# Last expert's sum in two half-column banks, and the first sixteen output rows taken straight from partial sums

## The chip, the core and the metric

The kernel runs on one core of a Trainium2 chip. A core has five engines with queues of their own: TensorE (PE: matmuls, with weight loads shown as PEld), VectorE (DVE), ScalarE (ACT), GpSimd (POOL) and SyncE (SP, which here only issues transfers). Matmul results go to PSUM, which has eight banks; everything else lies in SBUF. Sixteen transfer (DMA) engines move data between HBM and SBUF. The metric is the device time of one launch in microseconds (us); lower is better.

## What is computed

Two layers follow each other. The first is a gated recurrence over time, separately for each batch b and channel; the second a "soft mixture of experts" over all tokens of all batches:

```
B, S, D = 4, 5056, 256;  E = 8 experts, 4 slots each (32 slots), F = 1024
f = lb + (1 - lb) * sigmoid(f_logit)
h[t] = f[t] * h[t-1] + (1 - f[t]) * x[t]           # y = all h, [B*S, D]
logits = y @ phi                                    # [N, 32]
d = softmax of logits over the tokens
slot_input = d.T @ y                                # [32, D]
for e in range(8):
    hid = relu(slot_input[e] @ w1[e])               # [4, F]
    slot_out[e] = hid @ w2[e]                       # [4, D]
c = softmax of logits over the 32 slots
out = c @ slot_out                                  # [N, D], N = 20224
```

The output can't begin before slot_out is complete, since every output row is a mix of all 32 slots, and slot_out needs the last expert's w2.

## The kernel before

Nearly all of the span is one long pass over the input: 4 batches in groups of 512 time steps are loaded, gated (ScalarE), transposed (TensorE), scanned (VectorE), transposed back, and turned into exponentials of the logits, which stay in SBUF as `etall`: 128 partitions, 32 slots for each of the 4 batches, by 5056 time steps. The order of instructions on every engine is that in which the program is written (a manual schedule); a tile framework adds the waits. Weights are loaded by GpSimd's queue behind the input (`load_w`, L135), converted to bf16 on the way. The last w2 comes in two pieces: 6 of its 8 row blocks, then 2 (L144).

The part that the change touches begins after the pass.

- **Experts.** The 4 slots of an expert are rows of a 32-column block, since slots of all experts lie side by side. Eight row blocks (`fc`) of w2 are contracted one after the other. Experts 0 to 3 (L692 to L697) use `hid`, 32 columns wide: `fc % 4` picks one of four 32-row groups of PSUM, so that four matmuls can stand side by side in TensorE's array; the result is four partial sums, one in each row group. They are copied to `so4` (L699), and a matmul with `rep2` (L711), a 128x128 matrix of 4x4 identity blocks, adds the four groups up and leaves the sum four times, once in each group, as the output needs it (one copy of the slots for each batch). Experts 4 to 7 (L703 to L708) use `wide`, in which the 32 columns already stand four times; their matmuls are 128 columns wide and add into the same bank. `row_sums` (L407) and the reciprocals (L702, L716, L717) make the scale 1 / sum(c) of every output row. `spin` and `long_spin` (L150, L155) are matmuls whose result nobody reads; they keep TensorE busy.
- **slot_out and slot_bd.** When the last expert is in, VectorE copies the sum to bf16 as `slot_out` (L720). GpSimd multiplies it by two columns of `parity` into `slot_bd` (L722): for two batches at a time, each batch's slots in a block of their own, so that one matmul makes a row of both batches.
- **First output.** `pieces` (L765) makes the first 16 rows of batch 0's first block with `slot_out` (a "row" is 128 tokens, one on each partition): five transfers of 2, 2, 2, 4 and 6 rows, each row evicted from PSUM and scaled, half of them by ScalarE, half by VectorE. Then `by_rows` (L780) makes the last block, 7 rows, of two batches at a time with `slot_bd`, as tile `oc`: two transfers. `rest`, `whole` and `couple` make the remainder. All output transfers are issued by SP, in this order.

PSUM tiles of the first rows come from two pools, `psu` (2 banks) and `pfirst` (6 banks), by turns (`first_op`, L756). `ob_first` lies in a pool `ofirst` that is opened before the experts.

Of the kernel before, what the change touches and what calls it, by code (L numbers as in the profile page):

```python
# [9 lines left out]
F32 = mybir.dt.float32  # L10
# [8 lines left out]
def kernel(  # L19
# [148 lines left out]
    with tc.tile_pool(name="sp2", bufs=3) as sp2, \  # L168
# [433 lines left out]
        hid, wide = (ld.tile([P, 2, R, D], F32, name=i, tag="x_t") for i in ("hid", "wide"))  # L602
        hid = hid.rearrange("p u r d -> p (u r d)").bitcast(BF16)[:, ds(0, FC * E // 2 * NS)]
        wide = wide.rearrange("p u r d -> p (u r d)").bitcast(BF16)[:, ds(0, FC * E // 2 * P)]
        nc.gpsimd.memset(hid, 0.0)
        nc.gpsimd.memset(wide, 0.0)
        hid = hid.rearrange("p (f e s) -> p f e s", f=FC, s=NS)
        wide = wide.rearrange("p (f w b s) -> p f w b s", f=FC, b=B, s=NS)
# [29 lines left out]
    ob_first = ob_first[:, ds(0, wide_r * D)].rearrange("p (r d) -> p r d", d=D)  # L638

    with tc.tile_pool(name="ew", bufs=1) as ew, \  # L640
         tc.tile_pool(name="pm", bufs=2, space=PSUM) as pm, \
         tc.tile_pool(name="pbig", bufs=1, space=PSUM) as pbig:
# [27 lines left out]
        for q in range(E // Q):  # L670
            ht_ps = psu.tile([P, FC, P], BF16, name="ht_ps", tag="up")
            hi_v = his[q].rearrange("p (c f) -> p f c", f=FC)
            for fc in range(FC):
                nc.tensor.transpose(ht_ps[:, fc], hi_v[:, fc], ident)
            if q == 0:
                src = ht_ps.rearrange("p f (j s) -> p f j s", s=NS)[:, :, :, ds(0, SPE)]
                src = bass.AP(tensor=src.tensor, offset=src.offset,
                              ap=[list(src.ap[0]), [P, FC], [NS + SPE, Q], [1, SPE]])
                dst = hid[:, :, :, ds(0, SPE)]
                dst = bass.AP(tensor=dst.tensor, offset=dst.offset,  # L680
                              ap=[list(dst.ap[0]), [Q * NS, FC], [NS + SPE, Q], [1, SPE]])
                nc.scalar.copy(dst, src)
                continue
            for j in range(Q):
                s0 = (Q + j) * SPE
                src = ht_ps[:, :, ds(j * NS + s0, SPE)]
                copy = nc.scalar.copy if j % 2 == 0 else nc.vector.tensor_copy
                copy(wide[:, :, j, :, ds(s0, SPE)],
                     src.unsqueeze(2).broadcast_to([P, FC, B, SPE]))
        so4_ps = pm.tile([P, D], F32, name="so4_ps", tag="pm")  # L690
        for e in range(Q):
            for fc in range(FC):  # L692
                nc.tensor.matmul(so4_ps[ds(fc % 4 * NS, NS), :], hid[:, fc, e],
                                 w2_sb[e][:, fc],
                                 start=(e == 0 and fc < 4),
                                 stop=(e == Q - 1 and fc >= FC - 4),
                                 skip_group_check=True)  # L697
        so4 = ew.tile([P, D], F32, name="so4")
        nc.vector.tensor_copy(so4, so4_ps)  # L699
        so_ps = pm.tile([P, D], F32, name="so_ps", tag="pm")  # L700
        row_sums(1, range(4, 16))
        nc.vector.reciprocal(rrow[:, :wide_r], rs_ps[:, :wide_r])  # L702
        for j in range(Q):  # L703
            if j == 2:
                long_spin(tail[:, 1], 3)
            for fc in range(FC):
                nc.tensor.matmul(so_ps, wide[:, fc, j].rearrange("p b s -> p (b s)"),
                                 w2_sb[Q + j][:, fc], start=j == 0 and fc == 0,  # L708
                                 stop=j == Q - 1 and fc == FC - 1, skip_group_check=True)
            if j == 0:  # L710
                nc.tensor.matmul(so_ps, rep2, so4, start=False, stop=False,  # L711
                                 skip_group_check=True)
                row_sums(2)
            if j == 1:
# [186 lines left out]
```

## Time and profile before

| what | value |
|---|---|
| time, median of 3 runs | 196.53 us (196.46 to 196.62) |
| time of the profiled execution | 196.46 us |
| its span, first to last instruction | 194.7 us |
| busy: PE, DVE, ACT, POOL | 148.0, 142.1, 138.4, 102.5 us |
| HBM read, written | 58.23 MB, 20.71 MB |
| output transfers issued: five pieces, first oc, second oc | 143.36, 143.81, 144.29, 144.78, 145.82; 148.05; 150.35 us |
| slot_out copy (L720), slot_bd products (L722) | 0.42 us; 0.93 and 0.91 us |

The page of a profile shows busy times, the span in 40 slices (each digit is a busy share in tenths; PEclk is the granted TensorE clock; DMA is the transfer engines' share), and the chain of work that ended last, followed back from the last instruction. An answer of the timeline has start, length, engine, line, operation, tiles, shapes and count of each group of instructions, and in brackets how long the engine sat idle before it and what released it. SPq and POOLq are the queues that issue transfers. A window's row has its bounds and length, the busy time of PE, PEld, DVE, ACT and POOL with the instructions that were under way, then the granted clock, the transfer share and GB/s. Busy time of an engine that nobody waits for costs nothing.

### The profile page before, as it was taken

To read this page: it belongs to the slowest core of one execution; us is meant where nothing else is said; L and a number is where in the kernel's file an instruction comes from. 1 tells how busy PE (TensorE), PEld (TensorE's weight loads), DVE (VectorE), ACT (ScalarE), POOL (GpSimd) and SP (SyncE) were. 2 spreads that over 40 slices of the span, in tenths; PEclk is the share of its full clock that TensorE was granted. 3 is DMA by queue.
4 is the path that set the end of the run, shared out by engine and by line. 5 is a ranking of instruction groups with operands and counts; after the bars stand their busy time and mean duration, and the time that the engine had idled before them with its cause. 6 is when DMAs were issued, how large, how long until landed. Compare 5 with 4: busy or idle time off the path is not lost.

```text
span 194.7 us, 3260 instructions
## 1 busy us (share of the span) xinstructions
PE 148.0 (76%) x1216; PEld 105.2 (54%) x1216; DVE 142.1 (73%) x176; ACT 138.4 (71%) x192; POOL 102.5 (53%) x77
## 2 busy tenths in 40 slices
PE   0685686997989979898898976999696999980000
PEld 0474555685767758666685765667461764420000
DVE  2666899899799999999999999443178767770000
ACT  3687889799789998899998697421068688992000
POOL 2586877874998688884979977580030000000000
PEclk9999999699999999999999999999996555555555
DMA  5999999999999999999999999999939999999995
GB/s 200 418 434 423 428 428 421 431 431 356 373 426 426 405 338 423 426 428 344 391 412 398 269 221 213 214 215 214 177 149 425 432 447 431 431 431 431 431 431 222
DMA packets 11953, 70.75 MB, mean 363 GB/s; under 512 B 1297, under 2 KB 1682, under 8 KB 7458
## 3 DMA queue, kind: packets, MB, share of 16 engines
q1 hardware_dynamic: 9456, 62.13, 76.4%
q0 software_dynamic: 2480, 8.42, 21.6%
q8 instruction: 9, 0.15, 0.3%
q14 instruction: 6, 0.05, 0.1%
q10 hardware_dynamic: 2, 0.00, 0.0%
HBM read 58.23 MB, written 20.71 MB: 406 GB/s over the span
## 4 chain that ended last, share of the span: by engine, by line
PE 31%; DVE 23%; DMA 19%; ACT 6%; POOL 6%; issue 4%; SPq 1%; POOLq 1%; ACTq 0%; DVEq 0%
DVE h L334 16%; DMA w_t<-in_moe_w_dram 10%; PE op L829 7%; DMA w_sb<-in_moe_w_dram 6%; PE op L740 5%; POOL u_t L247 5%; PE hp L347 4%; PE up L266 4%; PE sp L251 4%; DMA f_t<-in_f_logit_dram 4%; DVE ht L366 3%; ACT s_t L236 3%; DVE oc L730 2%; PE lg L380 2%; PE slot_ps L185 1%
## 5 line engine op out<-in xcount | busy, mean ns | idle before, releaser
L247 POOL TENSOR_TENSOR u_t<-s_t,x_t 128x1024 bf16<-128x1024 bf16 (+1 forms) x39 | 82.3, 2127 | 21.7 <-ACT s_t L236 14.8
L334 DVE TENSOR_TENSOR_SCAN h<-a,h,up 128x512 bf16<-128x512 f32 x64 | 78.1, 1266 | 5.5 <-PE up L266 2.8
L236 ACT ACTIVATE s_t<-f_t 128x2048 bf16<-128x2048 f32 (+2 forms) x23 | 38.2, 1669 | 5.9 <-DMA f_t<-in_f_logit_dram 5.7
L347 PE MATMUL hp<-ident_f,h 128*128 128x128 f32 (+1 forms) x160 | 29.1, 305 | 7.4 <-DVE ht L366 4.7
L347 PEld LDWEIGHTS hp<-ident_f,h 128*128 128x128 f32 (+1 forms) x160 | 23.1, 206 | 16.4 <-DVE ht L366 9.3
L299 ACT ACTIVATE a<-sp,lbs 128x1024 f32<-128x1024 bf16 x28 | 29.7, 1114 | 2.2 <-PE sp L251 2.2
L251 PE MATMUL sp<-ident_f,s_t 128*128 128x128 f32 x144 | 21.4, 292 | 7.1 <-ACT s_t L236 5.7
L266 PE MATMUL up<-ident_f,u_t 64*128 64x64 f32 x224 | 21.2, 233 | 4.2 <-POOL u_t L247 4.0
L251 PEld LDWEIGHTS sp<-ident_f,s_t 128*128 128x128 f32 x144 | 17.4, 150 | 8.8 <-ACT s_t L236 6.7
L266 PEld LDWEIGHTS up<-ident_f,u_t 64*128 64x128 f32 x224 | 16.7, 141 | 8.9 <-POOL u_t L247 5.0
L366 ACT COPY ht<-hp 128x512 f32<-128x512 f32 (+1 forms) x21 | 12.2, 582 | 4.8 <-PE hp L347 4.8
L306 ACT ACTIVATE a<-sp,lbs 128x512 f32<-128x512 bf16 (+2 forms) x16 | 13.2, 867 | 2.6 <-PE sp L251 2.4
L185 PE MATMUL slot_ps<-rep,ident_f 128*128 128x256 f32 x42 | 13.8, 419 | 0.0
L366 DVE COPY ht<-hp 128x512 f32<-128x512 f32 (+1 forms) x19 | 12.7, 668 | 0.8 <-PE hp L347 0.8
L829 PE MATMUL op<-slot_bd,etall 64*128 64x512 bf16 x32 | 13.1, 626 | 0.0
L840 ACT ACTIVATE oc<-op,rrow 128x256 f32<-128x256 f32 x32 | 12.2, 486 | 0.8 <-PE op L829 0.3
L740 PE MATMUL op<-slot_out,etall 32*128 32x256 bf16 x64 | 12.6, 374 | 0.1
L834 DVE TENSOR_TENSOR oc<-op,rrow 128x1024 f32<-128x1024 f32 x8 | 9.7, 1223 | 3.3 <-PE op L829 3.3
L740 PEld LDWEIGHTS <-etall 32*128 32x128 bf16 x64 | 9.0, 153 | 3.9 <-issue 1.7
L734 ACT ACTIVATE ob<-op,rrow 128x256 f32<-128x256 f32 x24 | 9.4, 474 | 2.1 <-PE op L740 1.7
L380 PE MATMUL lg<-h,phi 128*32 128x512 bf16 (+1 forms) x80 | 10.5, 405 | 0.2 <-ACT et L404 0.2
L334 DVE TENSOR_TENSOR_SCAN h<-a,up 128x512 bf16<-128x512 f32 x8 | 9.3, 1208 | 1.6 <-PE up L251 0.9
(110 smaller groups left out, 170.0 us busy)
## 6 DMA issues: line engine op xcount, KB each, us to landing
f_t<-in_f_logit_dram SPq DMA_DIRECT2D x14, 1024.0 KB, 12.4
x_t<-in_x_dram SPq DMA_DIRECT2D x14, 1024.0 KB, 11.4
w_sb<-in_moe_w_dram POOLq DMA_DIRECT2D x14, 512.0 KB, 10.9
out_dram<-ob SPq DMA_DIRECT2D x3, 2048.0 KB, 9.7
f_t<-in_f_logit_dram SPq DMA_DIRECT2D x8, 512.0 KB, 8.6
x_t<-in_x_dram SPq DMA_DIRECT2D x8, 512.0 KB, 7.7
out_dram<-oc SPq DMA_DIRECT2D x1, 4096.0 KB, 13.9
out_dram<-oc SPq DMA_DIRECT2D x2, 2048.0 KB, 15.3
```

What stands on the lines that cost most here:

```text
L185: nc.tensor.matmul(slot_bank[:, 1], ident_f, wide_rep, start=first, stop=False, skip_group_check=True)
L236: nc.scalar.activation(s_t, f_t, ACT.Sigmoid, scale=-1.0)
L247: nc.gpsimd.tensor_tensor(uts[n][:, :r], s_t[:, :r], x_t[:, :r], ALU.mult)
L251: nc.tensor.transpose(ps[:, :, r], t[:, r].bitcast(F32), ident_f)
L266: nc.tensor.transpose(v[:, :, r], t(r)[k].bitcast(F32), ident_f[k, k])
L299: nc.scalar.activation(a, sp[:, :, :, :, o], ACT.Identity, scale=nomlb[:, ds(o, 1)], bias=1.0)
L334: nc.vector.tensor_tensor_scan(h[:, :T, o], decays[n // 2, o][:, n % 2, :T], up[:, :T, o], hs[number(g - 1, b)][:, ds(used(g - 1) - 1, 1), ...
L347: nc.tensor.transpose(hp[:n_p, r], hw[:, :n_p, r], ident_f)
L366: copy(hts[g][:n_p, b].rearrange("p r d -> p (r d)").bitcast(F32), hps.pop(n)[:n_p].rearrange("p r c -> p (r c)"))
L380: nc.tensor.matmul(lg[ds(b * NS, NS), :], phi[:, o], hs[number(g, b)][:, :T, o], start=o == 0, stop=o == DC - 1, skip_group_check=True)
L740: nc.tensor.matmul(op[:, j], ew[:, :, r + j], slot_out[ds(b * NS, NS)], start=True, stop=True, skip_group_check=True)
L829: nc.tensor.matmul(op[:, i_r].rearrange("p u d -> p (u d)"), ew[:, :, r + i_r], slot_bd[ds(j * 2 * NS, 2 * NS)].rearrange("s u d -> s (u d)"),
```

## The change

All eight experts now use the narrow `hid` (L604, L684); `wide` and `so4` are gone. Experts 0 to 6 add into the first half of bank `so_ps`, in four row groups. While weights are awaited, `fourfold` (L687) makes `four`: the exponentials of batch 0's first 2048 time steps, repeated in all four 32-row groups, by a matmul with `copies` (a bf16 copy of `rep`'s first 32 rows, made by GpSimd) and a copy to SBUF. With it, an output row of these 16 can be made from partial sums directly: the matmul over 128 partitions adds the four groups up.

The sum of experts 0 to 6 is copied by VectorE in bf16 (`parts[0]`) and in fp32 (`total`). The last expert goes to other PSUM columns by column halves: columns 0 to 127 into the second half of `so_ps`, columns 128 to 255 into another bank, `side_ps`. Its bf16 copy (`parts[1]`) is made half by VectorE, half by ScalarE; VectorE then adds both halves into `total`, and GpSimd copies `total` to bf16 (`parts[2]`).

Rows 0 to 3 come from two matmuls each, one with `parts[0]` and one with `parts[1]`, added in PSUM; rows 4 to 15 from one matmul with `parts[2]`. After the third piece TensorE adds up the four groups of `total` with `rep2` in fp32; after the fourth VectorE copies that to `slot_out`, and GpSimd makes `slot_bd` from it, as before. `by_rows` follows unchanged. On VectorE, in order: the half copy, two additions, rows 1, 3, 5, rows 8 and 9, `slot_out`, rows 13 and 14, row 15, then oc. On GpSimd: the copy of `total`, then the two products. SP's list of transfers is the same.

```diff
-        hid, wide = (ld.tile([P, 2, R, D], F32, name=i, tag="x_t") for i in ("hid", "wide"))
-        hid = hid.rearrange("p u r d -> p (u r d)").bitcast(BF16)[:, ds(0, FC * E // 2 * NS)]
-        wide = wide.rearrange("p u r d -> p (u r d)").bitcast(BF16)[:, ds(0, FC * E // 2 * P)]
+        hid = ld.tile([P, 2, R, D], F32, name="hid", tag="x_t")
+        hid = hid.rearrange("p u r d -> p (u r d)").bitcast(BF16)[:, ds(0, FC * E * NS)]
         nc.gpsimd.memset(hid, 0.0)
-        nc.gpsimd.memset(wide, 0.0)
...
+    four = ofirst.tile([P, P * wide_r], BF16, name="four")
+    parts = [ofirst.tile([P, D], BF16, name=f"parts{i}") for i in range(3)]
+    total = ofirst.tile([P, D], F32, name="total")
+    copies = ofirst.tile([P, P], BF16, name="copies")
+    nc.gpsimd.tensor_copy(copies[ds(0, NS)], rep[ds(0, NS)].rearrange("p b s -> p (b s)"))
...
+        def fourfold(i):
+            ps = psu.tile([P, G], F32, name="four_ps", tag="up")
+            nc.tensor.matmul(ps, copies[ds(0, NS)],
+                             etall[ds(0, NS), ds(i * G, G)], start=True, stop=True,
+                             skip_group_check=True)
+            copy = nc.scalar.copy if i % 2 == 0 else nc.vector.tensor_copy
+            copy(four[:, ds(i * G, G)], ps)
...
+        def expert(e):
             for fc in range(FC):
-                nc.tensor.matmul(so4_ps[ds(fc % 4 * NS, NS), :], hid[:, fc, e],
+                nc.tensor.matmul(so_ps[ds(fc % 4 * NS, NS), 0], hid[:, e // Q, fc, e % Q],
                                  w2_sb[e][:, fc],
...
+        def last_expert(fcs):
+            for o in range(DC):
+                for fc in fcs:
+                    nc.tensor.matmul(last_ps[o][ds(fc % 4 * NS, NS)], hid[:, 1, fc, Q - 1],
+                                     w2_sb[E - 1][:, fc, ds(o * P, P)],
+                                     start=fc < 4, stop=fc >= FC - 4, skip_group_check=True)
+
+        def add_last(o):
+            c = ds(o * P, P)
+            nc.vector.tensor_tensor(total[:, c], total[:, c], last_ps[o], ALU.add)
...
-        for j in range(Q):
-            if j == 2:
-                long_spin(tail[:, 1], 3)
+        for e in range(Q, E - 1):
+            if e == E - 2:
+                long_spin(tail[:, 1], 4)
+            expert(e)
+            if e == Q:
                 row_sums(2)
+                fourfold(0)
+                fourfold(1)
+                spin(tail[:, 1], 1, G)
+            if e == Q + 1:
...
+                fourfold(2)
+                fourfold(3)
+            if e == E - 2:
+                long_spin(tail[:, 1], 3)
+        nc.vector.tensor_copy(parts[0], so_ps[:, 0])
+        nc.vector.tensor_copy(total, so_ps[:, 0])
+        lanes = four.rearrange("s (p r) -> s p r", r=wide_r)
+
+        def direct(op, r, i):
+            nc.tensor.matmul(op, lanes[:, :, r], parts[i], start=i != 1, stop=i != 0,
+                             skip_group_check=True)
+
+        last_expert(range(FC - FC // 4))
+        ops = [psu.tile([P, 2, D], F32, name="op", tag="up") for _ in range(2)]
+        last_expert(range(FC - FC // 4, FC))
+        for r in range(2):
+            direct(ops[r][:, 0], r, 0)
+        spin(tail[:, 1], 1, D)
+        nc.vector.tensor_copy(parts[1][:, ds(0, P)], last_ps[0])
+        nc.scalar.copy(parts[1][:, ds(P, P)], last_ps[1])
+        add_last(0)
+        add_last(1)
+        nc.gpsimd.tensor_copy(parts[2], total)
-        ops = [psu.tile([P, 2, D], F32, name="op", tag="up")]
-        spin(ops[0].rearrange("p u d -> p (u d)"), 2, G)
-        nc.vector.tensor_copy(slot_out, so_ps)
-        for u in range(2):
-            nc.gpsimd.tensor_scalar_mul(slot_bd[:, u], slot_out, parity[:, ds(u, 1)])
...
-            for k in (1, 1, 1, 2, 3):
+            for step, k in enumerate((1, 1, 1, 2, 3)):
...
-                        share(op, i, b, r, n)
+                        for m in range(n):
+                            for p in ((1,), (0, 1), (2,))[min(r // 2, 2)]:
+                                direct(op[:, m], r + m, p)
...
+                if step == 2:
+                    sum_ps = first_op()[:, 0]
+                    nc.tensor.matmul(sum_ps, rep2, total, start=True, stop=True,
+                                     skip_group_check=True)
+                if step == 3:
+                    nc.vector.tensor_copy(slot_out, sum_ps)
+                    for u in range(2):
+                        nc.gpsimd.tensor_scalar_mul(slot_bd[:, u], slot_out, parity[:, ds(u, 1)])
```

## The prediction

> **What bounds the kernel now.** I read the slices of the page first, then the chain that ended last, then the timeline and the windows around the place where weights end and output begins. In the slices the transfer engines are full but for one slice (141.1 to 146.0 us), and after it the core writes at a steady 431 GB/s to the end:
>
> ```profile
> span 194.7 us, 3260 instructions
> ...
> PEclk9999999699999999999999999999996555555555
> DMA  5999999999999999999999999999939999999995
> GB/s 200 418 434 423 428 428 421 431 431 356 373 426 426 405 338 423 426 428 344 391 412 398 269 221 213 214 215 214 177 149 425 432 447 431 431 431 431 431 431 222
> ```
>
> So the span is: inputs and weights at transfer speed, a hole, 20.71 MB of output (the page counts 20.71 MB written) at transfer speed. The chain shows the hole: the last weights, their matmuls, slot_out, GpSimd's two products, and the first product rows that use them.
>
> ```profile
> 122.05 18.77 DMA w_t<-in_moe_w_dram
> ...
> 140.86 1.10 PE so_ps L707 x8
> ...
> 141.99 0.43 DVE slot_out L720
> ...
> 143.51 0.91 POOL slot_bd L722
> 144.43 0.04 issue
> 144.47 0.60 PE op L788 x2
> ```
>
> The timeline gives the issues of output transfers (SPq): five small ones from 143.36, the first large one (oc) at 148.05. It also shows GpSimd at work 142.59 to 144.42, and that VectorE and ScalarE reach the oc rows only at 145.41 and 145.63, after the small pieces.
>
> ```profile
> 142.59 1.83 POOL L722 TENSOR_SCALAR slot_bd<-slot_out,parity 128x256 bf16<-128x256 bf16 x2 [12.00 <-DVE slot_out L720]
> ...
> 143.36 2.79 SPq L777 DMA_DIRECT2D out_dram<-ob_first  x5
> ...
> 145.41 4.86 DVE L730 TENSOR_TENSOR oc<-op,rrow 128x512 f32<-128x512 f32 x8
> ...
> 145.63 4.53 ACT L795 ACTIVATE oc<-op,rrow 128x256 f32<-128x256 f32 x12
> ...
> 148.05 2.68 SPq L753 DMA_DIRECT2D out_dram<-oc  x2
> ```
>
> In windows of half a microsecond (busy time of each engine, granted clock, transfer share, GB/s) bytes move from 144.2 on and never stop; TensorE's clock is halved from 147.5:
>
> ```profile
> 143.50:144.00 0.50, 0.50 (x7) 0.50 (x6) 0.50 (x3) 0.50 (x3) 0.50 (x2) 1.00 0.00 0
> 144.00:144.50 0.50, 0.40 (x5) 0.29 (x4) 0.50 (x2) 0.50 (x2) 0.42 (x1) 1.00 0.57 221
> 147.50:148.00 0.50, 0.50 (x3) 0.17 (x2) 0.50 (x2) 0.50 (x3) 0.00 (x0) 0.50 1.05 434
> 149.00:149.50 0.50, 0.03 (x1) 0.00 (x0) 0.50 (x2) 0.50 (x3) 0.00 (x0) 0.50 1.02 424
> ```
>
> Two clocks follow. The stream starts at 144.21, 0.85 after the first issue. The five pieces hold 2.10 MB, which last 4.87 us at 0.431 MB/us, so the queue runs dry at 149.08 unless the oc transfer was issued by 148.23. It was issued at 148.05: **0.18 us in hand**. From there on the end is fixed by bytes. A change here is worth what it moves the first issue, less whatever dry time it opens before oc.
>
> **The change part by part.** The sum is made against the profiled execution (span 194.7, time 196.46; the median of the runs is 196.53, 0.07 more).
>
> Before the last weights. Removed: 32 full-width matmuls on `wide` (0.109 us apart), four copies into `wide`, the 3.53 us memset of `wide` (that of `hid` doubles, 0.97 more), the `so4` copy and its matmul. Added: 24 narrow matmuls for experts 4 to 6 (32 of that kind took 1.06), four `fourfold` matmuls of 512 columns (0.22 apart), their copies by ScalarE and VectorE (0.6 to 0.7 each), GpSimd's `copies` (0.29), two copies of the running sum (0.42 each) and 0.87 + 0.65 us of long_spin. All of it I cost at nothing. TensorE waits for weights at 136.59, 139.01 and 140.86, ScalarE is idle 9.8 us and VectorE 5.2 us before the end of this stage, and the weight loads are issued by GpSimd before the memset. The last of this work ends at about 140.3, 0.5 us before the weights it must not delay; if that cover were gone, the excess would fall on the first issue one for one.
>
> Last weights to first issue. The last two matmuls of before start at 141.57 and 141.68 and end at 141.95; four narrow ones of 128 columns (0.23 for a 128-column one, L413) end at about 141.85. The bf16 copy of 256 columns (0.42) becomes two of 128, side by side: VectorE's rows of 256 and 512 columns (0.416, 0.677) give 0.285 for 128, ScalarE's 128-column copy took 0.265. The bf16 sum is there at 142.16 instead of 142.41. TensorE follows 0.05 later, row 1 is evicted by VectorE from 142.62 instead of 142.88; the two additions into `total` (0.285 each, paced 0.21) stand ahead of it on VectorE but fit into the wait for that matmul. First issue 143.10 instead of 143.36: **0.26 earlier**.
>
> Rows 4 to 15. `total` is complete at 142.54. GpSimd starts 0.18 after VectorE ends (142.41 to 142.59 in before) and makes the bf16 copy. No row shows this copy; the nearest are 0.26 (L423, 64 columns), 0.285 (L86, 128 columns) and 0.92 (L722, 256 columns with a scalar). I take 0.4, near the copies: 0.285 and 128 more columns at the memset's 0.86 ns each. Bounds 0.26 and 0.92. TensorE then has rows 4 and 5 (0.11 each), the fp32 sum over the four row groups (two passes, 0.43 by L711: 135.03 to the next matmul at 135.47), and rows 6 to 9: the last starts at 144.15, and VectorE evicts rows 8 and 9 from 144.46.
>
> slot_out and slot_bd. `slot_out` now stands on VectorE behind that eviction (paced 0.60): 145.06 to 145.48. GpSimd's two products follow: 0.18 + 1.83 gives 147.49, and the first oc matmul is at 147.54 instead of 144.47. **That is 3.07 later**, while the stream began only 0.26 earlier. The products themselves may be shorter with nothing beside them: bounds 0.26 each (copies) and 0.92; I take what they took.
>
> The oc rows. Seven rows; four by VectorE (0.60 apart, 0.68 the last), three by ScalarE in two halves (0.356 apart). VectorE and ScalarE are through with the pieces by 146.5, so nothing is left to overlap with GpSimd. TensorE at half clock gives a row each 0.43 (L829's matmuls stand 0.43 apart): the seventh ends at 147.54 + 2.58 + 0.63 = 150.75, its eviction and the issue add 0.78: **oc issued at 151.53**. At full clock (0.215 apart) the evictions set the end: about 150.57.
>
> The sum. Dry time ends when oc's data start; against 148.23 that is 3.30 at half clock, 2.34 at full. The earlier first issue does not count any more, nor do the short gaps that late fourth and fifth pieces may open (issued at about 145.2 and 146.5): the stream waits for oc in either case. After oc the queue stays fed: the second oc issue comes 7 x 0.43 = 3.0 later and the transfer lasts 4.26. SP's queue has nothing else to send in between. So the end moves by 3.30: 196.46 + 3.30 = 199.76; I say **199.7**.
>
> [...] The profile's clock fell to half at 147.47, although TensorE had been busy 3.04 of the 3.42 us before. [...]
>
> **The rivals.**
> - The clock is still full through the oc rows. For it: the kernel holds full clock from 38.2 to 147.5 through many short pauses, and the moment of the fall need not be the same. Against it: it fell at 147.47 with more work around. Time: 196.46 + 2.34 = 198.8. A fall in the middle lies between.
> - GpSimd's two products are much cheaper alone, 0.26 each. For it: its copies. Against it: 0.92 twice in the only row. oc is issued 1.3 earlier than at full clock: 197.5.
> - Not slower: the stream is never dry, because slot_bd is ready by about 145.2, from where seven rows of evictions (2.6 to 3.0) still meet 148.2. For it: the pieces need slot_bd no more, and the sum is formed early. Against it: 145.2 is before VectorE even ends `slot_out` in my chain; 2.3 us would have to vanish. Then only the first issue counts: 196.2, or a little under if it is earlier than I think.
> - Slower still: the bf16 total takes 0.92 (0.5 later on the whole chain) with the clock halved: 200.3.
>
> **How the numbers follow.** Half clock 0.48, full clock 0.30, cheap products 0.06, not slower 0.10, slower still 0.06. A difference under 0.2% (0.4 us) can't be told from none here. The not-slower case I split evenly between faster by over 0.2% and within it; the others are all slower: 0.05, 0.05, 0.90. The range takes the half-clock, full-clock and slowest cases with a little around them: 198.4 to 200.5.
>
> **What would show it.** Right: the first small output issue near 143.1; GpSimd's copy of `total` near 142.7; slot_bd ending near 147.5; the first oc issue at 150.5 to 151.5; windows around 149 to 152 with a transfer share of 0; then 431 GB/s to the end. Wrong: slot_bd before 146; oc issued before 149; no empty window after 144; or the last weights landing at another time than 141.5, which nothing in the change should cause.

## The result, and the profile after

The changed kernel takes 200.14 us (median of 6 runs, 199.63 to 203.47), the kernel before on the same chip 196.55 (6 runs, 196.33 to 196.62): a ratio of 1.018, 95% interval 1.0161 to 1.0198. That is 3.6 us slower, near the 199.7 that was forecast. One of these runs (203.47) and two of a later kernel (202.90 and 203.72) fell in a slower state and are left out of the ratios, though not of the medians. The profiled execution took 200.58 us with a span of 198.7, against 196.46 and 194.7 before: 4.1 us more to explain.

The slices of the page after, to be laid beside those of before. The DMA row (busy share of the transfer engines in tenths) has one low slice, as before, and a 4 two slices on; in the GB/s row these are 55, the hole before the output, and 205, where before had 425.

```profile
span 198.7 us, 3303 instructions
...
PEclk9998799699999999999999999999995555555555
DMA  6999999999999999999999999999394999999992
GB/s 208 415 428 425 430 432 422 424 424 358 379 432 422 380 362 419 429 429 314 417 420 349 235 213 212 214 215 210 55 381 205 434 433 445 422 416 425 422 465 125
```

The chain that ended last, of the changed kernel, around the same place (start, length, what):

```profile
124.88 16.96 DMA w_t<-in_moe_w_dram
...
141.88 0.25 PE so_ps L712 x2
...
142.97 0.40 POOL parts L759
143.37 2.41 issue
...
146.76 0.91 POOL slot_bd L825
...
147.72 2.70 PE op L835 x11
150.41 3.08 DVE oc L767 x5
```

GpSimd's copy of `total` and its second product now both stand on it, with 2.41 us behind the copy in which GpSimd waits; the first oc matmul is at 147.72, where before had it at 144.47. The timeline has what fills that time: the small output issues (SPq, L816) start at 143.47, `slot_out` is made at 145.31, `slot_bd` ends at 147.67, and oc is issued at 151.23 instead of 148.05.

```profile
142.97 0.40 POOL L759 CAST parts<-total 128x256 bf16<-128x256 f32 x1 [14.31 <-DVE total L718]
...
143.47 3.59 SPq L816 DMA_DIRECT2D out_dram<-ob_first  x5
...
144.71 0.69 DVE L767 TENSOR_TENSOR ob_first<-op,rrow 128x512 f32<-128x512 f32 x1 [0.45 <-PE op L746]
...
145.31 0.41 DVE L823 CAST slot_out<-op 128x256 bf16<-128x256 f32 x1
...
145.84 1.83 POOL L825 TENSOR_SCALAR slot_bd<-slot_out,parity 128x256 bf16<-128x256 bf16 x2 [2.47 <-DVE slot_out L823]
147.72 3.94 PE L835 MATMUL op<-slot_bd,etall 64*128 64x512 bf16 x14 [2.39 <-POOL slot_bd L825]
...
151.23 2.72 SPq L790 DMA_DIRECT2D out_dram<-oc  x2
```

In windows of half a microsecond (bounds, length, busy time of PE, PEld, DVE, ACT, POOL, then granted clock, transfer share, GB/s) the pieces run out at 149.55 and the next bytes move from about 152.0. Between them the transfer engines have nothing for 2.5 us. The second group is the end: the bulk is through by 195.5, but a share of 0.08, which is little more than one engine of sixteen (0.0625), goes on to 197.0.

```profile
149.00:149.50 0.50, 0.50 (x6) 0.21 (x4) 0.41 (x1) 0.50 (x3) 0.00 (x0) 0.50 0.98 393
149.50:150.00 0.50, 0.50 (x6) 0.15 (x1) 0.45 (x1) 0.49 (x3) 0.00 (x0) 0.50 0.10 37
151.50:152.00 0.50, 0.16 (x1) 0.00 (x0) 0.50 (x2) 0.50 (x3) 0.00 (x0) 0.50 0.00 0
152.00:152.50 0.50, 0.00 (x0) 0.00 (x0) 0.50 (x2) 0.50 (x3) 0.00 (x0) 0.50 0.98 416
...
195.50:196.00 0.50, 0.00 (x0) 0.00 (x0) 0.00 (x0) 0.00 (x0) 0.00 (x0) 0.50 0.09 33
196.00:196.50 0.50, 0.00 (x0) 0.00 (x0) 0.00 (x0) 0.00 (x0) 0.00 (x0) 0.50 0.08 33
196.50:197.00 0.50, 0.00 (x0) 0.00 (x0) 0.00 (x0) 0.00 (x0) 0.00 (x0) 0.50 0.08 33
```

In the kernel before no engine is left alone like that; the windows show no more bytes from 193.0 on:

```profile
192.50:193.00 0.50, 0.00 (x0) 0.00 (x0) 0.00 (x0) 0.00 (x0) 0.00 (x0) 0.50 0.17 66
193.00:193.50 0.50, 0.00 (x0) 0.00 (x0) 0.00 (x0) 0.00 (x0) 0.00 (x0) 0.50 0.00 0
```

The trace gives the landings of the sixteen engines' shares of the last transfer. Before: fourteen at 192.93 to 193.06, then 193.54 and 193.74. After: fourteen at 195.84 to 195.97, then 196.43 and **197.79**. So the 4.05 us between the last landings are two things: the fourteen are 2.91 later, and the last engine, which was 0.68 behind the last of them in before, is now 1.82 behind, another 1.14. Of the 2.91, 2.5 is the empty stretch, 0.10 the later start of the stream (144.31, from 144.21), and about 0.2 the pieces themselves, which moved 404 GB/s between 144.5 and 149.5 where the same windows of before have 419.

A candidate for what holds one engine back stands in the page's section on the queues. The line of before had 9 and 0.15 MB; the changed kernel has:

```profile
q8 instruction: 10, 0.16, 0.3%
```

The page calls what this queue brings instructions. By the trace's transfer records each of its transfers is one packet of 16 KB and takes about 0.95 us (0.88 to 0.98 over both kernels). In before the ninth and last starts at 142.53, in the hole between weights and output. In the changed kernel the ninth starts at 141.16 and a tenth at 176.62, in the middle of the output. The records don't name an engine, so that a packet is on one engine, and that it is the one that lands last, is an inference, which the experiments test. The transfers go with TensorE's progress: when the ten start, TensorE has begun 222, 481, 734, 1002, 1264, 1474, 1799, 2060, 2230 and 2498 of its instructions, some 253 more each time in the mean. TensorE's rows in the trace (its instructions, a few of which may be missing) are 2468 before and 2504 after.

### The profile page after: what moved, and what is told of

It reads as the page before. It is cut to its first block, busy times and chain, and to the rows that moved or that the text cites. A ratio compares the mean times of both kernels' runs of the same rounds, so it can differ in the third digit from the quotient of the medians.

```text
span 198.7 us, 3303 instructions
## 1 busy us (share of the span) xinstructions
PE 149.8 (75%) x1233; PEld 105.4 (53%) x1234; DVE 144.6 (73%) x182; ACT 140.5 (71%) x195; POOL 100.5 (51%) x78
## 4 chain that ended last, share of the span: by engine, by line
PE 32%; DVE 24%; DMA 18%; ACT 8%; issue 4%; POOL 2%; SPq 1%; POOLq 1%; ACTq 0%
DVE h L334 15%; DMA w_t<-in_moe_w_dram 9%; PE op L876 7%; DMA w_sb<-in_moe_w_dram 6%; PE op L777 5%; PE sp L251 5%; PE hp L347 4%; PE up L266 4%; DVE ht L366 4%; DMA f_t<-in_f_logit_dram 4%; DVE h L321 3%; ACT s_t L236 2%; ACT a L299 2%; POOL u_t L247 2%; PE lg L380 2%
## 5 line engine op out<-in xcount | busy, mean ns | idle before, releaser
L236 ACT ACTIVATE s_t<-f_t 128x2048 bf16<-128x2048 f32 (+2 forms) x23 | 38.2, 1669 | 4.7 <-DMA f_t<-in_f_logit_dram 4.7
L251 PE MATMUL sp<-ident_f,s_t 128*128 128x128 f32 x144 | 22.1, 299 | 7.3 <-ACT s_t L236 5.9
L251 PEld LDWEIGHTS sp<-ident_f,s_t 128*128 128x128 f32 x144 | 18.0, 154 | 9.2 <-ACT s_t L236 6.9
L185 PE MATMUL slot_ps<-rep,ident_f 128*128 128x256 f32 x42 | 14.3, 431 | 0.0
L777 PE MATMUL op<-slot_out,etall 32*128 32x256 bf16 x48 | 10.7, 411 | 0.0
L321 DVE TENSOR_TENSOR_SCAN h<-a,h,up 128x224 bf16<-128x224 f32 x16 | 9.2, 657 | 0.0
```

Source lines behind the costliest of these rows:

```text
L236: nc.scalar.activation(s_t, f_t, ACT.Sigmoid, scale=-1.0)
L251: nc.tensor.transpose(ps[:, :, r], t[:, r].bitcast(F32), ident_f)
L321: nc.vector.tensor_tensor_scan(h[:, ds(t0, T), o], decays[n // 2, o][:, n % 2, ds(m * T, T)], up[:, ds(m * T, T), o], old[:, ds(t - 1, 1), ...
L777: nc.tensor.matmul(op[:, j], ew[:, :, r + j], slot_out[ds(b * NS, NS)], start=True, stop=True, skip_group_check=True)
```

## The experiments

Two theories had to be told apart for the 4.1 us. **Dry stream**: `slot_bd` is 3.2 us later, and the stream runs empty for what the pieces do not cover. **Tenth fetch**: a fetch of instructions falls into the output and delays one engine. The rivals were that something else holds the stream (the pieces' order, the halved clock) and that the late landing has nothing to do with the fetch.

### The fetch alone, on the kernel before

```diff
-                long_spin(tail[:, 1], 3)
+                spin(tail[:, 1], 22, NS)
```

Short unread matmuls in place of the long one, so that TensorE has more instructions; nothing else was meant to change.

> Theory F (fetch): of the 3.6 us that the changed kernel lost, some 1.4 come from a tenth fetch of 16 KB of TensorE's instructions (queue q8 shows 10 in place of 9), which falls into the output stream and makes one of the sixteen transfer engines end late. The kernel before, with 22 short unread matmuls in place of the long one ahead of expert 6 (40 TensorE instructions more, as long together, in a stretch where TensorE waits for weights), then shows 10 fetches on q8, a last stretch of about 1.4 us with a transfer share of 0.06, and takes 1.0 to 1.4 us more: 197.5 to 198.0. Rival (the number of instructions does not matter; the late end has another cause, such as later weights or the order of the transfers): 196.5, within 0.2.

Measured: 199.0 us (197.53 to 200.25), ratio 1.0123 (1.009 to 1.0155). The tenth fetch is there, at 176.4, and the last landing is at 197.56 with the one before it at 196.48: 1.08 behind. But the first output was issued at 146.10, 2.74 us late, and for that the trace shows two things. The ninth fetch came at 140.43, among the last weights, where before has it behind them. Of the sixteen engines' landings of the last weight transfer but one, fifteen are in by 140.77 and one comes at 142.44; in before all are in by 140.82. TensorE, which waits for that transfer, began at 142.48 instead of 140.86, 1.61 late. And without the long matmul the granted clock was halved from 141.84 to 145.25:

```profile
142.48 1.86 PE L707 MATMUL so_ps<-w_t,wide 128*128 128x256 bf16 x8 [2.49 <-DMA w_t<-in_moe_w_dram]
```

```profile
141.80:145.30 3.50, 2.46 (x10) 1.46 (x11) 0.42 (x1) 0.00 (x0) 0.32 (x1) 0.51 0.01 1
```

The kernel before has a granted clock of 1.00 in the same window. So this run shows a late engine together with a fetch twice, once at the end and once among the last weights, and its time is that of three things: the bulk of the engines lands 2.74 later (195.67), as much as the first issue, 1.61 of it from the late weights and the rest at half clock. That the missing long matmul cost the clock is likely but not shown: in two later kernels that keep the long ones (the last two below) the clock fell in this stage too.

### The same with the long matmul kept

```diff
                 long_spin(tail[:, 1], 3)
+                spin(tail[:, 1], 20, NS)
```

> The kernel before with 20 short unread matmuls (40 TensorE instructions) behind the long one ahead of expert 6, which stays, so that the clock is held this time. Theory F alone: q8 shows 10 fetches, one transfer engine lands 1.1 to 1.4 us after the others, the clock falls at about 147.5 as before: 197.4 to 197.8 against 196.4, and all runs close together. Rival (what the run with the long matmul taken out lost was the clock alone): 196.4.

Measured: 198.26 us, ratio 1.0106 (1.0069 to 1.0144), but scattered: 197.44, 197.48, 197.56, 197.96, 198.56, 199.07, 200.17, 200.35. Ten fetches. The profiled execution is the 200.35 one; there the clock was halved for longer in the pass (34.0 to 47.6 us, in before 34.8 to 38.2) and the last two matmuls on the last weights started at 144.45, 2.9 late; its last engine landed 0.92 after the one before it. The three lowest runs are 1.0 to 1.1 above before (196.48), about what the last engine was behind the next in the run above (1.08); they have no profile, so that this is all they are is argued, not shown. Why the runs above them scatter stays open.

### The changed kernel with fewer instructions

Some of the unread matmuls of the pass and the two short ones beside the experts are left out: 36 instructions of TensorE fewer.

```diff
-                    idle(2)
+                    idle(1)
...
-                elif 2 * B <= n < n_unit - 4 and n % (2 * B) in (1, 5, 6, 7):
+                elif 2 * B <= n < n_unit - 4 and n % (2 * B) in (1, 5, 7):
...
-                if n > 2 * B and n % (2 * B) == 3:
-                    idle(1)
...
-                spin(tail[:, 1], 1, G)
...
-        spin(tail[:, 1], 1, D)
```

> The changed kernel with 36 TensorE instructions fewer, all of unread matmuls (8 in the long pass, 2 at the end), which makes as many as the kernel before has. Theory F: 9 fetches on q8, no straggling engine at the end, the empty stretch before the first oc transfer unchanged: 1.2 to 1.4 us less than the changed kernel, 198.7 to 198.9. Rival: 200.1 as the changed kernel, or more if the clock falls in the pass for want of unread matmuls.

Measured: 202.32 us (199.56 to 203.72), ratio 1.0239 (1.0192 to 1.0286): slower in the median, not faster, with a scatter of 4 us whose lowest run is level with the lowest of the changed kernel. The mechanism is as expected, nine fetches and no engine alone at the end (fifteen at 199.11 to 199.25, one at 199.71). But in the profiled execution (202.39) the clock fell four times in the pass, 3.4 us each, where the changed kernel held it:

```profile
48.50:52.00 3.50, 3.50 (x26) 2.32 (x26) 2.20 (x2) 3.50 (x4) 3.50 (x2) 0.51 1.05 344
...
123.70:127.10 3.40, 3.40 (x27) 2.79 (x29) 2.48 (x4) 1.98 (x3) 3.40 (x7) 0.50 1.06 212
```

The same stretch of the changed kernel has 42 matmuls under way in place of 26, at the full clock:

```profile
48.50:52.00 3.50, 3.45 (x42) 2.50 (x43) 3.17 (x4) 3.50 (x4) 3.37 (x2) 1.00 1.03 328
```

The last weights' matmuls ran 3.7 us later (145.6), and that ate the gain. The place to save instructions was probably the wrong one; probably, because in two kernels whose pass is that of before the clock also fell where before held it (48.0 to 51.4 us with the products made twice, and the longer stretch above). The run has one clean reading for the prediction: here the clock was full until 157.8, and from the end of `slot_bd` (151.42) to the issue of oc (154.50) it took 3.08.

### The last expert in one bank

Instructions saved outside the pass: the last expert in 8 matmuls of full width into one bank instead of 16 of half width into two, and without the two short unread ones. TensorE has 2485 rows.

```diff
-        last_ps = [so_ps[:, 1, ds(0, P)], side_ps[:, ds(0, P)]]
+        last_ps = [so_ps[:, 1, ds(o * P, P)] for o in range(DC)]
...
-            for o in range(DC):
-                for fc in fcs:
-                    nc.tensor.matmul(last_ps[o][ds(fc % 4 * NS, NS)], hid[:, 1, fc, Q - 1],
-                                     w2_sb[E - 1][:, fc, ds(o * P, P)],
+            for fc in fcs:
+                nc.tensor.matmul(so_ps[ds(fc % 4 * NS, NS), 1], hid[:, 1, fc, Q - 1],
+                                 w2_sb[E - 1][:, fc],
...
-                spin(tail[:, 1], 1, G)
...
-        spin(tail[:, 1], 1, D)
```

> The changed kernel with the last expert's sum in one bank, all 256 columns of a matmul at once (8 matmuls in place of 16), and without the two short unread matmuls at the end: 20 TensorE instructions fewer, the long unread matmuls kept. Theory F: if 20 are enough, q8 shows 9 fetches, no engine ends late and the time falls by 1.1 to 1.4 from the changed kernel's 200.1, to about 198.9, or 199.1 since the two copies now share a bank and may wait for each other (0.2 to 0.3 on the first issue). If 20 are not enough, 200.1 to 200.4 with 10 fetches. Rival: no fall although q8 shows 9.

Measured: 199.33 us (199.01 to 199.87), ratio 1.0147 (1.0133 to 1.0161). The lines of this run:

```profile
142.06 0.29 DVE L752 CAST parts<-so_ps 128x128 bf16<-128x128 f32 x1 [1.52 <-PE so_ps L711]
142.39 0.27 ACT L753 CAST parts<-so_ps 128x128 bf16<-128x128 f32 x1 [4.08 <-DVE parts L752]
...
143.61 3.78 SPq L813 DMA_DIRECT2D out_dram<-ob_first  x5
...
146.17 1.83 POOL L822 TENSOR_SCALAR slot_bd<-slot_out,parity 128x256 bf16<-128x256 bf16 x2 [2.47 <-DVE slot_out L820]
...
151.08 2.72 SPq L787 DMA_DIRECT2D out_dram<-oc  x2
```

`slot_bd` and oc are as late as in the changed kernel, the stream is empty for 2.2 us, and yet the span is 197.2 instead of 198.7. There are nine fetches, and the end has no engine alone: fifteen land at 195.70 to 195.82, one at 196.30. Its last windows:

```profile
195.00:195.50 0.50, 0.00 (x0) 0.00 (x0) 0.00 (x0) 0.00 (x0) 0.00 (x0) 0.50 0.09 33
195.50:196.00 0.50, 0.00 (x0) 0.00 (x0) 0.00 (x0) 0.00 (x0) 0.00 (x0) 0.50 0.00 0
```

This bears out the second theory. The first engine of the bulk lands 0.14 before that of the changed kernel; the last one lands 1.49 before. That the one bank did it, and not the fetch, is ruled out by the last kernel below, which has two banks and nine fetches, and no late engine either.

The first two lines also show what two banks are for: in one bank ScalarE's half copy waits for VectorE's (released by `parts`, 0.33 later), and the first issue comes 1.87 after the last weights' matmuls start, against 1.585 with two.

### The dry stream alone, on the kernel before

GpSimd makes each product twice, so `slot_bd` is later and nothing else changes.

```diff
-        for u in range(2):
+        for u in (0, 1, 0, 1):
             nc.gpsimd.tensor_scalar_mul(slot_bd[:, u], slot_out, parity[:, ds(u, 1)])
```

> The kernel before with GpSimd's two products into slot_bd made twice over, so that slot_bd is ready 1.83 us later (146.26 by the profiled execution) and nothing else changes. Theory D: oc rows start at about 146.7 in place of 145.4, the first oc transfer is issued at about 149.4; the stream, which in the profiled execution had its last pieces through at about 149.5 and needs an issue 0.85 ahead of that, stays empty for 0.6 to 1.1 us, and the end is as much later: 197.0 to 197.5 against 196.4. Rival (the stream makes up for a late first oc transfer): 196.4.

Measured: 197.51 us (197.37 to 197.66), ratio 1.0051 (1.0039 to 1.0063). `slot_bd` ends 1.73 later (146.15), oc is issued 1.47 later, and a gap opens in the kernel that had none:

```profile
142.52 3.62 POOL L722 TENSOR_SCALAR slot_bd<-slot_out,parity 128x256 bf16<-128x256 bf16 x4 [12.00 <-DVE slot_out L720]
...
149.52 2.69 SPq L753 DMA_DIRECT2D out_dram<-oc  x2
```

```profile
149.00:149.50 0.50, 0.50 (x3) 0.15 (x2) 0.50 (x2) 0.50 (x3) 0.00 (x0) 0.50 0.35 139
149.50:150.00 0.50, 0.50 (x2) 0.15 (x1) 0.50 (x2) 0.50 (x2) 0.00 (x0) 0.50 0.00 0
150.00:150.50 0.50, 0.50 (x2) 0.00 (x0) 0.50 (x2) 0.50 (x3) 0.00 (x0) 0.50 0.34 143
```

The bulk lands 1.20 later (fifteen engines, 194.13 to 194.26), with nine fetches. So of 1.47 us of lateness at the issue of oc the pieces cover 0.27, and the rest falls on the end.

### The sum one step earlier

```diff
-                if step == 2:
+                if step == 1:
...
-                if step == 3:
+                if step == 2:
```

> The changed kernel with the fp32 sum of total made one piece earlier (before rows 4 and 5), slot_out copied after row 5 in place of after rows 8 and 9; GpSimd's products unchanged. Theory D (dry stream): slot_bd is ready about 1.05 us earlier, the first oc transfer is issued about 1.0 earlier and the empty stretch is as much shorter: 199.0 to 199.2, with q8 still at 10. Rival (the end is set by bytes, clock or fetch and not by the first oc transfer): 200.1 unchanged.

Measured: 199.84 us (198.70 to 201.11, four runs), ratio 1.0174 (1.0139 to 1.021); the median has more scatter than the effect. The profiled execution (199.37) is cleaner: `slot_bd` ends at 146.68 instead of 147.66, oc is issued at 150.13 instead of 151.23, the stream is empty for 1.48 us instead of 2.5, and the fourteen engines land 1.1 earlier (194.72 to 194.87). The tenth fetch is there, and the last engine lands at 196.68, 1.36 behind the one before it.

### Quicker products

ScalarE and VectorE make one half of `slot_bd` each, straight from PSUM; GpSimd makes `slot_out` as the sum of the two halves afterwards.

```diff
-                    nc.vector.tensor_copy(slot_out, sum_ps)
-                    for u in range(2):
-                        nc.gpsimd.tensor_scalar_mul(slot_bd[:, u], slot_out, parity[:, ds(u, 1)])
+                    nc.scalar.activation(slot_bd[:, 0], sum_ps, ACT.Copy, scale=parity[:, ds(0, 1)])
+                    nc.vector.tensor_scalar_mul(slot_bd[:, 1], sum_ps, parity[:, ds(1, 1)])
+                    nc.gpsimd.tensor_tensor(slot_out, slot_bd[:, 0], slot_bd[:, 1], ALU.add)
```

> The changed kernel with slot_bd made straight from the fp32 sum, one half by ScalarE and one by VectorE, at the same place in the order (after rows 8 and 9); GpSimd only adds the two halves into slot_out, which is needed later. Theory D: slot_bd is ready at about 145.8 in place of 147.7 (times of the profiled changed kernel), VectorE then ends the pieces at 146.7 and does the oc rows from there; first oc transfer issued about 2.0 earlier: 198.0 to 198.3. Rival: 200.1 unchanged, or more since ScalarE and VectorE take on 0.4 us each.

Measured: 198.58 us (198.53 to 198.70), ratio 1.011 (1.0097 to 1.0123), 0.3 above the range that was expected.

```profile
144.89 0.48 ACT L823 ACTIVATE slot_bd<-op,parity 128x256 bf16<-128x256 f32 x1
...
145.40 0.48 DVE L824 TENSOR_SCALAR slot_bd<-op,parity 128x256 bf16<-128x256 f32 x1 [0.33 <-ACT slot_bd L823]
...
149.34 2.72 SPq L790 DMA_DIRECT2D out_dram<-oc  x2
```

`slot_bd` ends at 145.88 in place of 147.66, and oc goes out 1.89 earlier. The fourteen land 1.90 earlier (193.94 to 194.09), the last engine at 195.89, 1.34 behind the one before it.

With these runs the issue of oc can be laid beside the end of the bulk, in the profiled executions (us later than in the kernel before: first oc issue, and the first landing of the bulk, fourteen or fifteen engines):

| kernel | oc issue | bulk lands | difference |
|---|---|---|---|
| products twice, in the kernel before | 1.47 | 1.20 | 0.27 |
| quicker products | 1.29 | 1.01 | 0.28 |
| sum one step earlier | 2.08 | 1.79 | 0.29 |
| one bank | 3.03 | 2.77 | 0.26 |
| the changed kernel | 3.18 | 2.91 | 0.27 |
| fewer instructions | 6.45 | 6.18 | 0.27 |

One line holds for all six, with nine fetches and with ten, at half clock and at full: where the stream runs dry before oc, the end of the bulk follows the issue of oc one for one, after the first 0.27 us. The two kernels before with more TensorE instructions are not in the table: there the stream did not run dry, and the bulk moved with the first issue (2.74 for 2.74, and 2.88 for 2.89). What the last engine adds is apart from it.

### Both, with nine fetches, and two tries to close the rest

One bank, the sum at the earlier step, and the quicker products together:

```diff
-                if step == 2:
+                if step == 1:
...
-                if step == 3:
-                    nc.vector.tensor_copy(slot_out, sum_ps)
...
+                if step == 2:
+                    nc.scalar.activation(slot_bd[:, 0], sum_ps, ACT.Copy, scale=parity[:, ds(0, 1)])
...
```

> The last kernel with both cures for slot_bd: the fp32 sum before rows 4 and 5, and slot_bd straight from it by ScalarE and VectorE after row 5. Theory D: slot_bd is ready about 2.7 us earlier than in the changed kernel (145.0 by its times), the oc rows start where VectorE and ScalarE end the pieces (146.3), the first oc transfer is issued at about 149.0 and the stream is empty for at most 0.3 us. With 9 fetches 196.4 to 196.8, with 10 197.6 to 198.0. Rival: something else in the change holds it at 199 or more.

Measured: 197.39 us (197.33 to 198.87), ratio 1.0071 (1.0046 to 1.0096), above the 196.4 to 196.8 that was expected with nine fetches. With the fetch gone and `slot_bd` at 145.40, 2.7 us of the 3.6 are back. Its oc issue is 1.40 later than that of before, its bulk lands 1.12 later (194.05), 0.28 less, as in the table. In the windows, though, most of the empty time is not right before oc:

```profile
146.00:146.50 0.50, 0.50 (x4) 0.30 (x3) 0.50 (x1) 0.50 (x2) 0.15 (x1) 1.00 0.91 332
146.50:147.00 0.50, 0.50 (x5) 0.17 (x4) 0.50 (x3) 0.50 (x3) 0.00 (x0) 1.00 0.33 123
150.00:150.50 0.50, 0.00 (x0) 0.00 (x0) 0.50 (x2) 0.50 (x3) 0.00 (x0) 1.00 0.55 227
```

0.38 us are empty between 146.0 and 147.0, and bytes move again at 146.9, which is 0.85 us after the fourth piece was issued (146.06; 145.46 in the changed kernel, 144.78 in before). In the program the sum's matmul and the two products now stand ahead of that piece's rows on TensorE, ScalarE and VectorE. 0.22 are empty at 150.0, before oc. The next kernel goes for the second of these alone, by the first oc transfer in two parts, rows 0 to 3 and 4 to 6.

```diff
-            both(i, j, ob)
+                if j == 0 and r in (n_r // 2, n_r - 1):
+                    r0 = 0 if r < n_r - 1 else n_r // 2 + 1
+                    dst = out.rearrange("(b t) d -> b t d", b=B)[ds(0, 2), ds(t0, P * n_r)]
+                    nc.sync.dma_start(
+                        out=dst.rearrange("u (p r) d -> p u r d", r=n_r)[:, :, ds(r0, r + 1 - r0)],
+                        in_=ob[:, :, ds(r0, r + 1 - r0)])
+            if j:
+                both(i, j, ob)
```

> The one-bank kernel with the sum and the quick products early (197.39), and its first oc transfer in two, rows 0 to 3 and rows 4 to 6. Dry-stream theory: the first part can be issued three rows' evictions, about 1.3 us, before 149.45, which is before the pieces are through, so the 0.67 us of empty stream go and nothing else changes: 196.7 (196.5 to 197.0), nine instruction fetches, no empty window after 144.5. Rival, the stream is not the limit between 147 and 150 but something that the earlier sum itself costs: 197.4 as without the split.

Measured: 197.66 us (197.49 to 200.06, 12 runs), ratio 1.0067 (1.0038 to 1.0096): no gain, the expectation was wrong. The gap before oc did go, but the larger one ahead of the fourth piece (issued at 146.86) is still there, and it now is what the stream loses:

```profile
147.00:147.50 0.50, 0.50 (x3) 0.21 (x2) 0.50 (x2) 0.50 (x3) 0.00 (x0) 1.00 0.16 41
147.50:148.00 0.50, 0.50 (x4) 0.26 (x3) 0.50 (x2) 0.50 (x3) 0.00 (x0) 1.00 0.63 254
```

In this execution the clock was also halved from 137.2 to 144.0, and the first issue came at 144.08 instead of 143.52, so its gaps stand 0.6 later than those of the run above.

The second try has, beside that, the last expert in two banks again (the lines of the one-bank diff undone, the short unread matmuls still left out):

```diff
-        last_ps = [so_ps[:, 1, ds(o * P, P)] for o in range(DC)]
+        last_ps = [so_ps[:, 1, ds(0, P)], side_ps[:, ds(0, P)]]
```

> As the kernel above, with the last expert's sum in two banks by column halves again (16 narrow matmuls in place of 8): the change without what it adds behind its rows 4 to 15. Two theories meet. The two banks bring the first issue 0.2 to 0.3 us earlier than one bank does: 196.4 if TensorE's stream still takes nine instruction fetches. With ten (it has some 16 instructions and as many weight loads more, and ten were seen from 2504 rows of TensorE on, nine up to 2486) the last of them falls in the output and holds one transfer engine back by about 1.0 to 1.4 us: 197.5 to 197.8, with landings of the last transfer in which one is over 1 us behind the others. Rival, the late landing has another cause than the fetch: no late landing in spite of ten, or one in spite of nine.

Measured: 197.90 us (197.21 to 199.43, 12 runs), ratio 1.0082 (1.0049 to 1.0115). It has nine fetches at 2501 rows of TensorE, so the tenth begins between 2501 and 2504, as far as the trace's rows are complete, and no engine is far behind (fifteen at 193.90 to 194.16, one at 194.55). So of the two theories the fetch's was right about the landings, but the 196.4 that it gave for nine fetches was wrong by 1.5. The gap ahead of the fourth piece stays. The clock was halved from 138.0 to 141.4, and the first issue came at 143.58, no earlier than with one bank. No version was faster than the kernel before.

## Why the prediction was right, step by step

**The direction and its mechanism: shown.** The prediction said that the pieces no longer need `slot_bd` early but that oc does, so that a `slot_bd` 3 us later opens an empty stretch. `slot_bd` ended at 147.66 (forecast 147.49), the first oc matmul stood at 147.72 (147.54), and the stream was empty from 149.55 to 152.0. Doubling the products in the kernel before gave the same gap without the rest of the change, and making `slot_bd` earlier in the changed kernel moved the bulk's end by as much as it moved oc's issue (1.12 for 1.10, 1.90 for 1.89).

**Last weights to first issue: right in the interval, not in the clock time.** Forecast 0.26 earlier. From the last weights' first matmul to the first issue it took 1.585 us instead of 1.79, 0.2 less. The half copies took 0.29 and 0.27 (forecast 0.285 and 0.265). In the clock of the execution the first issue came 0.11 later, since the weights arrived 0.31 later, a difference that the prediction said nothing in the change should cause. In the profiled executions whose clock held up to there those matmuls start between 141.50 and 141.88, and the changed kernel with nothing but quicker products has 141.56; so I take it for scatter, which no run here settles.

**GpSimd's copy: right.** 0.397 us, forecast 0.4 between bounds of 0.26 and 0.92. The products took 1.83 together, as before. The second, from 146.75, had no work of VectorE or ScalarE beside it from 146.66 on and still took 0.91: the rival that they are cheap alone is refuted.

**The oc rows: the size lay between the forecast and its rival.** The forecast was 4.04 us from `slot_bd` to the issue at half clock, 3.08 at full clock. Measured: 3.57. The clock fell at 148.25, in the middle of the rows, where before it fell at 147.47. The two executions in which it held through nearly all the rows, and in which the rows waited for `slot_bd` alone (fewer instructions, one bank), give 3.08 and 3.08, exactly the full-clock sum. The rival for the full clock was thus right about its own price, and the case in the middle, which the prediction named, came about.

**The dry time: right but for its size.** The forecast was that the end moves by what oc's issue is later, less 0.18 us in hand: 3.30. The rule is that of the table; in hand were 0.27. The pieces' windows were at 419 GB/s in before, not at the 431 that I took from the later stream. So the bulk moved 3.18 - 0.27 = 2.91: of the 0.39 too much, 0.30 is oc's issue, forecast at 151.53 and seen at 151.23 (its rows 0.47 shorter, for the clock, and `slot_bd` 0.17 later), and 0.09 the cover.

**Before the last weights: wrong.** "All of it I cost at nothing" was the step that failed. The engines' cover for that work held: TensorE still waited 0.62 and 0.29 us for the last two transfers of weights. What I did not count was the instructions themselves. With 36 more rows of TensorE (2504, from 2468) came a tenth fetch, at 176.62, in the output stream, where there is no cover, and one of sixteen engines landed 0.9 to 1.4 us behind the next in every profiled kernel that has it there (five). The page of before has the line with the nine fetches; it took no part in my sum. Without this the profiled execution would have taken about 196.46 + 2.91 = 199.4; it took 200.58 (200.14 in the median). So the forecast for the bulk, 199.76, was 0.4 too high, and 1.1 was left out at the end; that 199.7 came so close to the median is in part luck, the one taking from the other.

**The clock.** The half-clock stretches that end within a profiled execution are 3.4 us long, or 6.8 or 13.6 in two of the runs above. The trace's clock records of before start at 14.35, 34.83, 38.24 and 147.47, which are 20.480, 3.413 and 109.226 us apart (6, 1 and 32 times 3.413); those of the changed kernel start at 15.13, 18.54, 21.96, 35.61, 39.02 and 148.25, which are 3.413, 3.413, 13.653, 3.413 and 109.226 apart (1, 1, 4, 1 and 32 times). The fall in the output was at 147.47 in before, at 148.25 in the changed kernel and at 150.15 in the one with one bank, though their output started within 0.25 us of each other (143.36, 143.47, 143.61). TensorE was busy 3.02, 1.02 and 2.12 us of the 3.41 before these falls. Here are the three windows, of the changed kernel, of the one with one bank, and of the kernel before:

```profile
144.84:148.25 3.41, 1.02 (x8) 0.74 (x7) 1.95 (x5) 1.58 (x5) 1.83 (x2) 1.00 1.05 407
```

```profile
146.75:150.17 3.42, 2.12 (x11) 1.17 (x11) 1.95 (x4) 1.50 (x6) 1.25 (x2) 1.00 0.92 367
```

```profile
144.06:147.47 3.41, 3.02 (x14) 1.41 (x13) 3.41 (x7) 3.41 (x11) 0.36 (x1) 1.00 1.01 398
```

Busy time alone does not order them: in the run with fewer instructions a window with 1.48 us busy (147.60 to 151.00) was followed by no fall, with a granted clock of 1.00 to 157.80. What makes the clock fall stays open; a halved clock through all the oc rows was my estimate from the one fall in before.

## What to carry to other kernels

When output is bound by transfers, a change to what feeds it is judged at each transfer in the list, not at the first one: getting the first rows out earlier is worth nothing if a later, larger transfer waits for what was put behind them (here the first issue came 0.2 us sooner after the last weights, oc was issued 3.18 later, and the bulk landed 2.91 later). Instructions are traffic too: look at the instruction queue's line before adding some, however well they are hidden. With a tenth fetch in the output one engine of sixteen landed 1.36 us behind the next here, and with one among the last weights an engine landed 1.67 behind the others, and TensorE, which waited for that transfer, began 1.61 late. And before taking unread matmuls out, see what clock the windows around them have: with 36 instructions fewer two stretches of 3.4 us had 0.51 and 0.50 where the changed kernel has 1.00.

## What the runs showed of the hardware that was not expected

- By the transfer records of these traces a fetch of instructions is one packet of 16 KB and took about 0.95 us (0.88 to 1.07). In every profiled kernel that had one in the output (five of them) one engine landed 0.9 to 1.4 us behind the next; where there was none, the last engine was at most 0.5 behind the next. Nine fetches were seen up to 2501 rows of TensorE, ten from 2504 on; the tenth started when TensorE had begun 2498 to 2503, so with its last instructions. A fetch among the last weights went with one engine 1.67 us behind the others. Why the delay is longer than the fetch stays open.
- Unread matmuls in the pass seem to carry the clock: with 36 instructions of TensorE fewer it fell four times, 3.41 us each (0.51 from 48.50 to 52.00, where the changed kernel has 1.00), and the last weights' matmuls were 3.7 us later. That is one profiled execution; one such fall, at 48.0, was also seen in a kernel with its pass unchanged, the changed kernel has two in its own pass, at 18.54 and 35.61, and before has one, at 34.83.
- One evicting engine waited for the other where both read the same bank: ScalarE's copy started 0.33 us after VectorE's in one bank, 0.05 after it in two. Whether chip or framework asks for that wait, no run here tells.
- The small pieces moved 419 GB/s in the kernel before and 404 in the changed one (means of the windows from 144.5 to 149.5), while the stream behind them holds 431 in before.
